# A state-space and GEGLU kernel: first weights' loads set free, constant products in TensorE's planned idle time, and a new list of priorities

## The chip, the core and the metric

The kernel runs on one core of a Trainium2 chip. The engines of the core that matter here are TensorE (PE: matrix products, which write to PSUM), VectorE (DVE), ScalarE (ACT: functions from a table that has to be loaded before a function of another table can be used) and the issuers of transfers: SyncE (SP) above all, ACT and GpSimd (POOL) for a few. Each engine works through its own list of instructions in order; an instruction that has to wait holds up everything behind it on that engine. The metric is the time of one execution on the device, in microseconds (us).

## The reference

A block on 2048 tokens with 448 channels. It is conditioned: six rows of 448 numbers come from a vector `c`.

```
mod = (silu(c) @ w_mod) -> sa, ca, ga, sb, cb, gb        # six modulation rows
h = layernorm(x) * (1 + ca) + sa
x = x + ga * S4(h)                                       # long convolution per channel
h = layernorm(x) * (1 + cb) + sb
x = x + gb * GEGLU(h)                                    # (gelu(h @ w_gate) * (h @ w_up)) @ w_down, 448 -> 1792 -> 448

S4: K[d, l] = Re sum_n C[d,n] exp(dt[d] A[d,n] l) dt[d] B[d,n]   # 256 complex terms, l = 0..2047
    y[l, d] = sum_k K[d, k] h[l - k, d] + Dskip[d] h[l, d]       # by FFT of length 4096
```

## The kernel before

**Stages.** The kernel first works up the parameters of S4 (`prep`, four groups of 112 channels): logarithms and angles of the 256 terms, split in pieces of bf16 and put in DRAM (`lh_d`), from which they come back as tables `lt`. From a table, TensorE forms exponents and angles (`x.mm`, `y.mm` in `exps`; `angles`), ACT takes exponentials and sines, DVE multiplies magnitudes with sines (`mults`), and TensorE contracts over the 256 terms (`kgen`). This goes on for 56 tiles of 8 channels; `ktail` (L735 and around) turns each pair of tiles into the first stage of a Fourier transform. Meanwhile the input is normalized with the modulation rows (`mod_row`, products at L768; `u_norm_a`, products at L832) and transformed in two stages (`u_stage_b`, L895), by way of DRAM. Channels go in three groups (160, 160, 128). For each group, `k_fft`, and `t_fft` for the last, multiply the transforms and go back; the result goes to DRAM (`y_d`) and comes back token by token (`yi`). `conv_out` finishes the inverse transform (`co.mm`, L1246 and L1251), adds the input, normalizes, and transposes (`co.t`, L1294 and L1296, for the first of four blocks of 512 tokens). Then `gate_up` (L1365, L1371) and `down_first`/`down` (L1441, L1472) do the GEGLU in products of f16 parts, each number as a high and a low part.

**Weights.** `weight(cb, k, v)` loads half `k` of chunk `cb` of the gate and up weights (512 KB) into one of three tiles `w`, and ACT and DVE split it into f16 parts (`w.hi`, L1195; `w.lo`, L1199 and L1200). The loads of chunk 0 wait for the end of the generating stage (`EV["end"]`, when its memory is given back) and for the store of the third of nine pieces of the last group (`YO[2, 2]`); the others wait for all loads of the first block's convolution output (`YL`).

**What sets the order.** Nothing is ordered by hand. Each piece of work is a task: `add(name, {engine: planned us}, due time, function, tasks it depends on, buffers it takes, buffers it uses)`. `Plan.order()` simulates the engines with these planned durations: it takes the engine that can start first, looks at all tasks which could start there within a quarter of a microsecond of that, and takes the one with the lowest due time. A tile of work has due times one apart, from 0 to 56. To a task that needs ACT to change its function table the constant `STICK` is added, so that it is put off. `spread()` adds to each due time an offset by the task's name from the list `LEAD` (several values: the tasks of the name in order are cut into as many parts); the list `LEAN` holds offsets for the choice between ACT and DVE where a task can run on either. `Plan.run()` then issues the tasks in the order found, each engine's list in that order, and the machine runs them with semaphores between the engines. A buffer given back late, a transfer or a slow product shifts the real times, but never the order.

The functions that the change touches:

Of the kernel before, what the change touches and what calls it, by code (L numbers as in the profile page):

```python
# [23 lines left out]
L, D, N, FF = 2048, 448, 256, 1792  # L24
# [15 lines left out]
    "anc": (-49.265, -80.499, -3.124, -78.469, -116.66, -66.369),  # L40
    "ang": (-3.269, -2.827, -2.729, -3.205, -2.925, -2.697), "bn": (42.111, 82.157, 5.194, -204.331),
    "c.ai": (71.008,), "c.ak": (31.634,), "c.au": (64.741,), "c.ea": (129.571,), "c.id": (-5.74,), "c.ih": (81.5,),
    "c.ld": (-70.212,), "c.rd": (36.588,), "co.add": (126.534,), "co.adde": (-479.654,), "co.addl": (177.332,),
    "co.addx": (510.429, 276.254, 263.838, 306.027), "co.c2": (-16.462, 185.363, 68.605, 81.504),
    "co.h": (1287.071, 1321.404), "co.h2": (-57.238, -19.565, -34.416, 62.618), "co.l": (166.825, 99.971),
    "co.l2": (-304.102, -376.884, -381.167, -327.959), "co.mm": (1047.13,), "co.mme": (35.95,),
    "co.mml": (321.391,), "co.mmx": (504.891, 504.282, 510.751, 509.801), "co.n": (-32.018, -300.752),
    "co.nx": (-309.183, -245.328, -200.245, -90.738), "co.rc": (52.991, 384.121), "co.rcx": (915.491,),
    "co.rt": (-12.141, 45.958), "co.rtx": (-618.711,), "co.t": (505.324, 339.683),
    "co.t2": (-464.884, -636.939, -578.467, -639.884),  # L50
    "cos": (-96.053, -141.432, -54.911, -135.117, -68.696, -62.333),
# [6 lines left out]
    "dt": (81.074,), "e.f": (-100.312, 117.922), "e.hi": (227.13, 344.995), "e.ld": (-39.805, -1.088),  # L58
    "e.lo": (8.272, -319.182), "ev.end": (-23.435,), "ev.fp": (-187.94,), "ev.geg": (-67.509,), "ev.ub": (109.206,),
    "f.fc": (-74.649, -73.839, -55.611, 15.224, 63.434, 91.147),  # L60
    "f.fwd": (58.743, 8.62, -112.416, 150.202, 15.302, 243.705),
    "f.inv": (36.676, 5.254, 29.465, 109.483, 81.689, 3.388),
    "f.pr": (-67.219, -99.593, -75.227, -57.007, -57.18, -110.784),
    "f.st": (28.45, 6.08, 190.379, 150.17, -1.775, -10.415),
    "f.ut": (-73.325, -24.751, 34.463, 33.094, 102.931, 195.732),
    "f.z": (-23.585, -5.38, 134.288, 63.022, -67.177, -41.953), "gs": (138.291,),
    "gu": (497.845, 500.786, 503.249, 509.096, 515.626, 545.649),
    "gu.g": (-625.109, -552.414, -602.197, -714.965, -686.389, -501.12), "gu.h0": (645.72, 522.69),
    "gu.ha": (-729.389, -596.515, -731.42, -528.62, -704.301, -709.342),
    "gu.hs": (-239.586, -121.625, -135.62, -164.459, -9.293, -189.977), "gu.l0": (-16.693, -130.465),  # L70
    "gu.la": (-265.608, -410.165, -336.957, -514.583, -455.359, -305.327),
    "gu.ls": (191.831, 190.571, 255.197, 314.456, 219.503, 228.103),
    "gu.m": (114.811, 93.18, 25.848, 285.848, 134.211, 151.44),
# [8 lines left out]
    "kev": (9.96, 92.747, 141.711, 161.609, -130.449, 155.883),  # L82
    "kgen": (64.902, 22.754, 68.327, 70.484, 152.571, 111.028),
    "kout": (-13.486, 89.933, 39.546, 40.541, 35.588, -116.335), "lt0": (111.543, 130.526),
    "lt1": (47.626, 207.789), "m.ev": (47.089, 10.526), "m.ld": (6.556, 99.682), "m.mm": (63.997, 73.516),
    "mag": (65.374, -12.18, 200.812, 142.622, 59.432, 179.295), "norm": (-89.669, 35.116, -31.629, -46.135),
# [7 lines left out]
    "pad": (46.718,), "rcp": (1.165,), "rstd": (-51.788,), "silu": (45.884,),  # L94
    "sin": (110.019, -92.652, 19.55, -44.113, 102.58, 38.168),
    "sin2": (46.891, 86.759, 111.859, -3.781, 88.196, 21.274), "t.fc": (52.17, 4.168), "t.fwd": (-57.224, -139.59),
    "t.inv": (-32.42, 14.481), "t.p0": (-56.821, 45.808), "t.p1": (-115.221, 1.658, 219.974, -99.911),
    "t.st": (5.684, 132.896), "t.u": (-64.85, -19.41), "t.z": (101.922, 155.786),
    "tx": (-52.929, -36.943, 40.099, -29.624, 27.922, 13.415),
    "tyc": (3.154, 41.689, 41.884, -19.547, 61.093, 75.57),  # L100
    "tys": (-48.605, -173.627, -88.574, -42.524, 36.217, -71.751), "ua": (-84.287, -53.971, -196.44, -59.869),
    "ua.ev": (-107.017, -68.693, 4.26, 84.323, 6.479, 38.324), "ua.st": (-38.083, -30.78, 73.606, -86.939),
    "ub": (61.829, 6.214, 28.274, 40.439, 45.706, 57.504),
    "ub.ev": (19.991, 47.119, -27.71, 3.763, 47.267, -78.016), "ub.fc": (-145.241, 235.998),
    "ub.st": (171.069, 76.93), "ub.u": (-80.805, 32.953), "w.hi": (47.827, -108.842, 52.672, -16.405),
    "w.ld": (-16.684, 35.68, 34.326, 174.065), "w.lo": (33.536, 32.676, -41.147, -28.811), "warm": (-47.271,),
    "wr.ld": (118.569, -172.29, -6.657, 0.537, 11.936, 73.483), "wr.st": (-77.265, -16.436),
    "x.exp": (-46.635, 7.137, 2.518, -127.479, -61.616, -65.308), "x.ld": (-9.142,), "x.ld0": (-42.934,),
    "x.ld1": (-8.964,), "x.mm": (-1.652, -1.606, -1.613, -1.701, -1.664, -1.631), "x1.ld": (17.13, -239.16),
    "y.exp": (29.939, 99.375, 54.648, -1.232, -161.973, 74.141),  # L110
    "y.mm": (-1.933, -1.54, -1.223, -1.275, -1.525, -1.518), "yi.d00": (-147.672,), "yi.d01": (-171.741,),
    "yi.d10": (-130.853,), "yi.d11": (-32.365,), "yi.e": (-88.98,), "yi.l0": (-123.965, 88.548),
    "yi.l1": (-88.669, -10.274), "yi.ld": (196.171,),
}
LEAN = {
# [23 lines left out]
class Task:  # L139
    def __init__(self, n, eng, v, fn, deps, alloc, table, kb):  # L140
# [6 lines left out]
        for b in alloc:  # L147
            self.need[b.tag] = self.need.get(b.tag, 0) + 1


class Plan:


    TABLE, HOP, STICK, RATE = 1.3, 0.3, 121.096, 280.0
    WAIT = {"ACT": 0.0}

    def __init__(self, slots):
        self.slots, self.given = slots, {t: [] for t in slots}
        self.tasks = []

# [189 lines left out]
def s4_geglu(ctx: ExitStack, tc: tile.TileContext, a: dict, out: bass.AP):  # L350
# [342 lines left out]
    KGT = {}  # L693
# [950 lines left out]
```

## Time and profile before

| | us |
|---|---|
| median of 3 runs | 823.77 |
| lowest, highest | 823.62, 831.2 |
| profiled execution, own time | 825.18 |
| profiled execution, span from first to last instruction | 823.4 |
| PE busy | 748.4 (91%) |
| DVE busy | 599.6 (73%) |
| ACT busy | 470.3 (57%) |

The mean granted clock of TensorE in the profiled execution is 0.969 of full speed. How to read the rows below: a row of a group or of the timeline gives the source line, the engine, the operation, the tile written and the tiles read, and the shapes; `x24` is a count of instructions. `[3.26 <-issue]` is the time that the engine had been idle before the row and what ended it; "issue" means nothing that the profile shows. A product of f32 operands is shown as two instructions. PEld is TensorE's loading of the stationary operand, which overlaps products. SPq, ACTq and POOLq are the issuing of transfers by these engines. In the chain of waits (the work that ended last, followed back) a row is a start, a length and what it was.

### The profile page before, as it was taken

How to read it: one execution, taken by the hardware profiler on the slowest of the kernel's cores; microseconds unless marked ns; L12 is line 12 of the kernel's file. 1: busy time of each engine (PE TensorE's matmuls, PEld its weight loads, DVE VectorE, ACT ScalarE, POOL GpSimd, SP SyncE). 2: the span in 40 equal slices, each digit the busy share in tenths (PEclk: the TensorE clock that was granted, in tenths of full speed). 3: DMA queues.
4: the chain of work that ended last, by engine and by line, in shares of the span. 5: the costliest groups of instructions: out<-in, count | busy, mean ns of one | idle time of the engine just before them, and what ended most of it. 6: DMA issues, size and time to landing. Idle time of an engine off the chain costs nothing.

```text
span 823.4 us, 19059 instructions
## 1 busy us (share of the span) xinstructions
PE 748.4 (91%) x8166; PEld 461.2 (56%) x8166; DVE 599.6 (73%) x981; ACT 470.3 (57%) x629; POOL 6.0 (1%) x14
## 2 busy tenths in 40 slices
PE   2786789999799999998589999999999999999997
PEld 1344344444577767778466445444496445864477
DVE  7789998999889989897494783178863686244542
ACT  5598999899968999971244553034442353113320
POOL 0000000000000000000200000000000000000000
PEclk9888799999999999999889999999999999999999
DMA  9552369996858846899669756245315322022101
GB/s 283 148 167 92 105 189 236 285 273 200 236 146 257 233 133 193 253 307 295 189 197 298 267 179 179 75 140 166 117 53 146 135 91 90 34 79 90 45 12 35
DMA packets 92526, 136.83 MB, mean 166 GB/s; under 512 B 21280, under 2 KB 75200, under 8 KB 92442
## 3 DMA queue, kind: packets, MB, share of 16 engines
q1 hardware_dynamic: 89514, 133.75, 53.8%
q10 hardware_dynamic: 2608, 1.61, 0.8%
q8 instruction: 64, 1.05, 0.5%
q0 software_dynamic: 320, 0.26, 0.1%
q14 instruction: 20, 0.16, 0.1%
HBM read 100.48 MB, written 36.01 MB: 166 GB/s over the span
## 4 chain that ended last, share of the span: by engine, by line
PE 67%; ACT 12%; DVE 10%; DMA 6%; issue 3%; SPq 1%; DVEq 0%; ACTq 0%
PE pq L1371 30%; PE pq L1472 9%; PE pd L1441 3%; PE kg L710 3%; ACT fg L643 2%; PE pg L630 2%; PE pf L999 2%; PE pq L1365 2%; PE pf L768 2%; ACT my L617 2%; PE pf L1085 2%; PE pf L895 2%; DVE tx L679 2%; DMA fg<-in_w_mod 2%; PE pd L1472 1%
## 5 line engine op out<-in xcount | busy, mean ns | idle before, releaser
L1371 PE MATMUL pq<-ht,wr 128*128 128x512 f16 (+1 forms) x1200 | 250.0, 367 | 0.0
L1371 PEld LDWEIGHTS <-wr 128*128 128x128 f16 x1200 | 115.4, 98 | 128.6 <-issue 11.0
L1378 ACT ACTIVATE ge<-pq 128x512 f32<-128x512 f32 (+1 forms) x60 | 33.9, 568 | 144.5 <-PE pq L1365 93.9
L1385 DVE TENSOR_TENSOR fq<-ge,pq 128x512 f32<-128x512 f32 (+1 forms) x60 | 38.5, 649 | 72.1 <-PE pq L1371 48.2
L1397 ACT ACTIVATE hh<-fq 128x1024 f16<-128x1024 f32 (+1 forms) x49 | 47.1, 963 | 54.5 <-DVE fq L1385 41.8
L1472 PE MATMUL pq<-d,hh 128*128 128x224 f16 x504 | 73.2, 259 | 0.0
L710 PE MATMUL kg<-ty,tx 128*32 128x64 f32 x3584 | 61.8, 221 | 11.3 <-DVE ty L687 6.4
L679 DVE TENSOR_TENSOR tx<-mx,fg 128x1024 f32<-128x1024 f32 x56 | 68.0, 1220 | 4.0 <-ACT fg L654 2.2
L683 DVE TENSOR_TENSOR ty<-my,fg 128x1024 f32<-128x1024 f32 x56 | 68.2, 1219 | 3.0 <-PE kg L710 2.8
L710 PEld LDWEIGHTS kg<-ty,tx 128*32 128x32 f32 x3584 | 53.0, 110 | 27.6 <-issue 11.2
L1472 PE MATMUL pq<-d,hlo 128*128 128x224 f16 x252 | 65.3, 259 | 0.0
L1400 DVE TENSOR_TENSOR hlo<-fq,hh 128x1024 f16<-128x1024 f32 (+1 forms) x49 | 53.9, 1104 | 5.3 <-ACT hh L1397 5.0
L643 ACT ACTIVATE fg<-pg 128x1024 f32<-128x1024 f32 x56 | 56.6, 1019 | 1.9 <-issue 1.2
L1472 PEld LDWEIGHTS <-hh 128*128 128x128 f16 x588 | 56.7, 98 | 1.1 <-issue 0.4
L617 ACT ACTIVATE my<-pg 128x1024 f32<-128x1024 f32 x56 | 55.3, 1041 | 3.1 <-PE pg L612 2.9
L999 PE MATMUL pf<-q,fc 128*128 128x160 f32 x264 | 42.9, 313 | 0.3 <-DVE q L989 0.3
L630 PEld LDWEIGHTS <-lt 64*128 64x128 bf16 x336 | 20.7, 95 | 37.4 <-issue 20.7
L999 PEld LDWEIGHTS pf<-q,fc 128*128 128x128 f32 x264 | 37.7, 195 | 6.3 <-issue 3.3
L630 PE MATMUL pg<-ea,lt 64*128 64x512 bf16 x168 | 34.9, 389 | 6.2 <-ACT fg L643 4.4
L687 DVE TENSOR_TENSOR ty<-my,fg 128x512 f32<-128x512 f32 x56 | 38.4, 686 | 0.0
L686 DVE SCALAR_TENSOR_TENSOR ty<-my,fg 128x512 f32<-128x512 f32 x56 | 38.4, 685 | 0.0
L735 PE MATMUL kg<-ak,ke 128*64 128x128 f32 x448 | 32.1, 284 | 6.2 <-DVE ke L730 4.4
(172 smaller groups left out, 1196.3 us busy)
## 6 DMA issues: line engine op xcount, KB each, us to landing
wr<-w_d SPq DMA_DIRECT2D x21, 896.0 KB
fc<-in_k_fc SPq DMA_DIRECT2D x20, 576.0 KB
u_d<-so SPq DMA_DIRECT2D x32, 224.0 KB
w<-in_wgu SPq DMA_DIRECT2D x14, 512.0 KB
ui<-u_d SPq DMA_DIRECT2D x10, 672.0 KB
w_d<-wr SPq DMA_DIRECT2D x7, 896.0 KB
fq<-in_wd SPq DMA_DIRECT2D x14, 448.0 KB
us<-uo SPq DMA_DIRECT2D x22, 240.0 KB
```

The source lines that it names most:

```text
L617: A.activation(yb.tile.rearrange("p a b c -> p (a b c)"), pb.tile, AF.Exp)
L630: T.matmul(pa[:, nh * 512:nh * 512 + 512], w, x, start=(k == 0), stop=(k == 2))
L643: A.activation(fb.tile[:, 0].rearrange("p x (n k) -> p n x k", n=2), pb.tile.rearrange("p (n x k) -> p n x k", n=2, x=2), AF.Sin, scale=TW ...
L679: V.tensor_mul(tx.tile, xb.tile[:, xm, None, :].to_broadcast([128, 2, 512]), fb.tile[:, :, 0])
L683: V.tensor_mul(ty.tile[:, 1], yb.tile, fy()[:, 1, :, None, :].to_broadcast([128, 16, 2, 32]))
L710: T.matmul(kg[32 * g:32 * g + 32, 2 * (s % 2) + q, :64], tx[:, r, nh, 4 * q + g], ty[:, r, nh, 4 * q + g], start=(r == 0 and nh == 0), sto ...
L999: T.matmul(pz.tile[:, e % 32 - sl0], fc.tile[:, i, 1 + t], pp.tile[:, t, i], start=(t == 0 and e != 32), stop=(t == 1 and e != 0))
L1371: T.matmul(pb[k].tile[:, ts], wr.tile[:, 4 * lo + t, k, c0:c0 + 128], ht[:, m, ts], start=f % 2 == 0 and i == 0, stop=f % 2 == 1 and i == 9)
L1385: V.tensor_mul(to if half is None else to[:, half:half + 1], *src)
L1397: A.activation(hg.tile[0][:, cb, c], fq.tile[:, c], AF.Copy)
L1400: V.tensor_sub(hg.tile[1][:, cb, c], fq.tile[:, c], hg.tile[0][:, cb, c])
L1472: T.matmul(bank(k)[:, m], x[:, p, q[0], ts], w[:, p, q[1]], start=new and m == 0 and p == 0 and z == 0, skip_group_check=True, stop=i in ( ...
```

## The change

Three things are changed.

First, the loads of weight chunk 0 no longer wait for the store of the third piece of the last group; they wait for the end of the generating stage alone.

Second, `Plan.run()` notes for each TensorE task how long the plan has TensorE idle before it (its planned start less the planned end of the TensorE task before). A new function `spin` runs at the beginning of six kinds of tasks: the exponents of `x.mm`, the even tiles of `kgen`, the modulation rows `m.mm`, the first transform of the input `ua`, the inverse transform `co.mm` and the transposition `co.t`. It multiplies a constant (the 1e-5 in `small`, broadcast to 128x128 and to 128x448 in f32) into the PSUM tile that the task writes anyway, as often as 0.78 us (for 448 columns) go into the planned idle time less 1.5 us. The real products of the task then start that tile anew, so the numbers are not changed.

Third, all values of `LEAD` and `LEAN` are new (some 330 numbers), and `STICK` goes from 121.096 to 68.223.

```diff
 LEAD = {
-    "anc": (-49.265, -80.499, -3.124, -78.469, -116.66, -66.369),
-    "ang": (-3.269, -2.827, -2.729, -3.205, -2.925, -2.697), "bn": (42.111, 82.157, 5.194, -204.331),
+    "anc": (-33.662, -127.623, -27.273, -157.195, -251.708, -72.885),
+    "ang": (-2.669, -2.583, -2.453, -2.632, -2.559, -2.718), "bn": (39.589, -6.152, 5.448, -202.784),
...
-    "x.exp": (-46.635, 7.137, 2.518, -127.479, -61.616, -65.308), "x.ld": (-9.142,), "x.ld0": (-42.934,),
-    "x.ld1": (-8.964,), "x.mm": (-1.652, -1.606, -1.613, -1.701, -1.664, -1.631), "x1.ld": (17.13, -239.16),
+    "x.exp": (-2.362, 27.057, -3.169, -158.186, 25.842, -71.775), "x.ld": (80.516,), "x.ld0": (-45.034,),
+    "x.ld1": (-29.649,), "x.mm": (-1.578, -1.384, -0.684, -1.385, -1.425, -1.155), "x1.ld": (126.383, -240.404),
...
 class Plan:
-    TABLE, HOP, STICK, RATE = 1.3, 0.3, 121.096, 280.0
+    TABLE, HOP, STICK, RATE = 1.3, 0.3, 68.223, 280.0
...
     def run(self):
+        free = 0.0
         for t in self.order():
+            if t.on == "PE":
+                t.idle, free = t.start - free, t.start + t.eng["PE"]
             t.fn(t.on) if len(t.eng) > 1 else t.fn()
...
+    def spin(me, dst, w=D):
+        for _ in range(int(max(0.0, me[0].idle - 1.5) / (0.78 * w / D))):
+            T.matmul(dst, eps.to_broadcast([128, 128]), eps.to_broadcast([128, w]), start=True, stop=True)
...
         def mm():
             pb.tile = fft.tile([128, D], FT, name="pf")
+            spin(me, pb.tile)
             for t in range(4):
                 T.matmul(pb.tile, c_sb[:, t:t + 1].to_broadcast([DT, 128]), wb.tile[:, t], start=(t == 0), stop=(t == 3))
...
         t2 = add("m.mm", {"PE": 3.22}, v, mm, [t1, t_si], [pb], [wb])
+        me.append(t2)
...
-        hold = [YO[2, 2]] if cb < 1 else YL
+        hold = [] if cb < 1 else YL
         t1 = add("w.ld", {"SP": 0.42}, v - 3, ld, [EV["end"]] + hold, [wb], kb=540)
...
                     if i == 0:
                         pb.tile = POOLS["pd"].tile([128, D], FT, name="pd")
+                    spin(me, pb.tile[:, c0:c1], c1 - c0)
```

In `x.mm`, `kgen`, `ua` and `co.t` the call stands in the same way right after the PSUM tile is taken, with 448 columns. In `co.mm` it is as wide as the part of the tile that the task writes (320, 128 or 448 columns).

More of the change, by code (lines that the diff above doesn't have):

```diff
@@ L45 @@
[L45 to L50, printed above, removed]
@@ L64 @@
[L64 to L70, printed above, removed]
@@ new lines @@
+    "c.ai": (101.027,), "c.ak": (51.722,), "c.au": (99.561,), "c.ea": (166.012,), "c.id": (-139.636,),
+    "c.ih": (99.349,), "c.ld": (-111.229,), "c.rd": (34.126,), "co.add": (212.033,), "co.adde": (-451.647,),
+    "co.addl": (214.941,), "co.addx": (383.522, 332.612, 197.427, 173.233),
+    "co.c2": (-4.423, 230.15, -17.347, 23.461), "co.h": (1272.011, 1283.454),
+    "co.h2": (-135.097, -190.215, -25.533, 9.464), "co.l": (41.666, 122.947),
+    "co.l2": (-239.239, -340.178, -513.762, -355.004), "co.mm": (1081.405,), "co.mme": (13.439,),
@@ new lines @@
+    "e.lo": (73.412, -325.804), "ev.end": (30.652,), "ev.fp": (-421.684,), "ev.geg": (-34.16,), "ev.ub": (13.47,),
+    "f.fc": (-73.936, -73.769, -11.85, 1.571, 13.444, 40.743),
+    "f.fwd": (50.686, -9.55, -79.473, 68.866, 75.039, 267.068),
+    "f.inv": (31.32, 15.273, 27.125, 42.942, 7.704, 10.82),
+    "f.pr": (-29.69, -89.709, -108.076, -161.126, -21.4, -65.159),
+    "f.st": (23.073, 80.857, 222.835, 174.159, -46.499, 51.897),
+    "f.ut": (-73.466, -8.761, 21.784, 68.205, 83.502, 144.889),
@@ new lines @@
+    "f.z": (10.584, 18.046, 60.685, 42.739, -117.035, 2.404), "gs": (281.067,),
+    "gu": (483.796, 504.978, 502.422, 517.711, 492.364, 538.942),
+    "gu.g": (-641.228, -487.117, -586.793, -843.942, -558.876, -526.773), "gu.h0": (676.217, 477.898),
+    "gu.ha": (-653.183, -638.161, -685.036, -501.963, -686.837, -740.305),
+    "gu.hs": (-254.496, -129.449, -206.502, -147.449, -41.548, -76.458), "gu.l0": (90.866, -195.141),
+    "gu.la": (-123.506, -257.422, -386.797, -503.762, -370.765, -243.05),
@@ new lines @@
+    "w.ld": (1.251, 10.186, 42.098, 313.892), "w.lo": (28.842, 98.808, -7.712, -66.755), "warm": (-39.422,),
+    "wr.ld": (84.303, -194.951, 103.092, -69.821, -11.301, 59.36), "wr.st": (-81.84, -85.079),
+    "x.exp": (-2.362, 27.057, -3.169, -158.186, 25.842, -71.775), "x.ld": (80.516,), "x.ld0": (-45.034,),
+    "x.ld1": (-29.649,), "x.mm": (-1.578, -1.384, -0.684, -1.385, -1.425, -1.155), "x1.ld": (126.383, -240.404),
+    "y.exp": (32.326, 75.885, 82.416, -34.586, -96.967, -56.007),
+    "y.mm": (-1.65, -1.332, -0.716, -1.386, -0.969, -0.964), "yi.d00": (-61.494,), "yi.d01": (-166.546,),
@@ L587, in exps, with xmm @@
             pb, mb = Buf("pg"), Buf("mx")
-            def xmm(grp=grp, pb=pb):
+            me = []
+            def xmm(grp=grp, pb=pb, me=me):
                 pb.tile = gen.tile([128, 1024], FT, name="pg")
+                spin(me, pb.tile[:, :D])
                 for m, s in enumerate(grp):
@@ L695, in kgen @@
     def kgen(s, deps):
-        m = s // 2
+        m, me = s // 2, []
         if s % 2 == 0:
@@ L702, in go @@
                 KG[m].tile = kgp.tile([128, 4, 128], FT, name="kg")
+                spin(me, KG[m].tile.rearrange("p q d -> p (q d)")[:, :D])
             kg = KG[m].tile
@@ L712, in go @@
                                      tile_position=(0, 32 * g))
-        return add("kgen", {"PE": 1.04}, s, go, list(deps) + [KGT.get(s - 1) if s % 2 else None],
-                   [KG[m]] if s % 2 == 0 else [], [TX[s], TY[s]] + ([KG[m]] if s % 2 else []))
+        me.append(add("kgen", {"PE": 1.04}, s, go, list(deps) + [KGT.get(s - 1) if s % 2 else None],
+                      [KG[m]] if s % 2 == 0 else [], [TX[s], TY[s]] + ([KG[m]] if s % 2 else [])))
+        return me[0]
     AKB = [Buf("ak%d" % (g % 2)) for g in range(3)]
@@ L826, in u_norm_a, with mm @@
             pbs = [Buf("pf"), Buf("pf")]
-            def mm(j=j, pbs=pbs):
+            me = []
+            def mm(j=j, pbs=pbs, me=me):
                 for h in range(2):
                     pbs[h].tile = fft.tile([128, D], FT, name="pf")
+                spin(me, pbs[0].tile)
                 for h in range(2):
@@ L1289, in norm, with tr @@
                 V.scalar_tensor_tensor(xn.tile, xn.tile, RS[blk][:, j:j + 1], sb, op0=OP.mult, op1=OP.add)
-            def tr(pt=pt, xn=xn):
+            me = []
+            def tr(pt=pt, xn=xn, me=me):
                 pt.tile = POOLS["ps"].tile([128, 4, 128], FT, name="pq")
+                spin(me, pt.tile.rearrange("p k t -> p (k t)")[:, :D])
                 for k in range(3):
```

79 lines of the change are left out of this document (38 added, 41 removed), and 48 rows, old and new, of tables (LEAD, LEAN).

## The prediction

> **What bounds the kernel now.** I began with the page: how full TensorE is, where its clock drops, who carries the chain that ended last.
>
> ```profile
> span 823.4 us, 19059 instructions
> PE   2786789999799999998589999999999999999997
> PEclk9888799999999999999889999999999999999999
> PE 67%; ACT 12%; DVE 10%; DMA 6%; issue 3%; SPq 1%; DVEq 0%; ACTq 0%
> ```
>
> A slice is 20.6 us. TensorE is nearly full from slice 22 on. Its clock is below full in three places: slices 2 to 5, slices 20 and 21 (from about 400 us), and a dip in the slices before 240 us. I then split the span at five events: the first table arrives (33.2), the last kernel tile is done (376.5), the last inverse transform ends (398.6), the first gate/up product starts (421.5).
>
> ```profile
> 0.00:33.20 33.20, 13.41 (x28) 6.05 (x28) 23.14 (x60) 16.32 (x28) 0.20 (x4) 0.99 0.82 237
> 33.20:376.50 343.30, 306.10 (x5306) 194.49 (x5306) 313.17 (x468) 308.00 (x396) 0.00 (x0) 0.95 0.71 207
> 398.60:421.50 22.90, 9.84 (x66) 6.15 (x64) 14.47 (x32) 8.40 (x14) 2.82 (x5) 0.77 0.58 187
> 421.50:823.40 401.90, 396.97 (x2574) 232.44 (x2572) 231.53 (x396) 131.98 (x184) 0.00 (x0) 0.99 0.38 120
> ```
>
> Columns: stretch, its length, busy time (and instructions) of PE, weight loads, DVE, ACT and POOL, granted clock, DMA share, GB/s. The last stretch is TensorE's: 396.97 of 401.90 us at clock 0.99, so no order and no constant product can shorten it by more than 5 us. Whatever the change brings or costs falls ahead of 421.5 us. In the long stretch three engines are about equally full: DVE is idle for 343.3 - 313.2 = 30.1 us, ACT for 35.3, PE for 37.2. There the order decides, and DVE's 30 us is the most that a better order can win. The first and third stretches are chains in which each engine waits for another.
>
> **The constant products at the start.** The spin loop stands ahead of the real products in TensorE's queue and waits for nothing but the PSUM tile and the constant. The first host is the product of a modulation row.
>
> ```profile
> 2.63 13.19 DMA fg<-in_w_mod
> 15.96 12.27 PE pf L768 x24
> 28.33 4.86 DMA lt<-lh_d
> 233.23 3.01 PE pf L768 x8
> ...
> 15.96 12.26 PE L768 MATMUL pf<-fg,pk 112*128 112x448 f32 x24 [15.96 <-DMA fg<-in_w_mod]
> 21.32 0.34 PEld L768 LDWEIGHTS pf<-fg,pk 112*128 112x128 f32 x1 [0.41 <-issue]
> 22.04 0.19 PEld L768 LDWEIGHTS pf<-fg,pk 112*128 112x128 f32 x1 [0.38 <-issue]
> 22.24 0.54 ACT L771 ACTIVATE rows<-pf 128x448 f32<-128x448 f32 x1 [6.01 <-PE pf L768]
> 22.30 0.34 ACTq L520 DMA_DIRECT2D lh_d<-lh  x1
> 22.41 0.19 PEld L768 LDWEIGHTS pf<-fg,pk 112*128 112x128 f32 x1 [0.19 <-issue]
> ```
>
> The first four rows are the chain of waits (start, length), the others the timeline. Three modulation rows took 12.27 us at the start; one took 3.01 us at 233 us, so three warm ones take 9.03. The weight loads show why: they start 0.72 us apart up to 22.04 and 0.37 apart after it. From 15.96 to 22.04, 6.1 us, the array ran at half speed. Being warm at 15.96 is worth 12.27 - 9.03 = 3.2 us, and this lies on the path: ACT waits 6.01 us for the first of these rows with the store of the first factor queued behind it, and the load of the first table is issued at 28.33, when the last of the rows is out.
>
> How many constant products are planned I can't read; I put the real idle time in place of the planned one. 15.96 us give int((15.96 - 1.5) / 0.78) = 18. One is a quarter of a modulation row: 3.01 / 4 = 0.75 us warm, 1.5 cold. Four run in the 6.1 us of warming, the other 14 take 10.5, together 16.6 us; begun near 1 us they end at 17.5, 1.6 us after the data landed (2.63 + 13.19 = 15.82). So the term lies between -3.2 (they fit) and -1.6 (they overhang); I take -2.5.
>
> The Trainium skill, "TensorE: Matmul & The Clock Gate", Part 1, says that the array is held at half clock until it has been busy for about one window of 3.4 us. The trace has the same two speeds but needed 6.1 us here; by the page's figure the warm start would be worth 3.4 / 2 = 1.7 us (estimate), by the row 3.2, and the row decides.
>
> **The next cold stretches.**
>
> ```profile
> 31.48 1.16 PE L832 MATMUL pf<-xt,au 64*128 64x448 f32 x4 [3.26 <-issue]
> 43.49 1.92 PE L832 MATMUL pf<-xt,au 64*128 64x448 f32 x4
> 64.01 1.00 PE L832 MATMUL pf<-xt,au 64*128 64x448 f32 x4
> 78.98 1.98 PE L735 MATMUL kg<-ak,ke 128*64 128x128 f32 x16 [3.75 <-DVE ke L730]
> ...
> 34.63 1.49 PE pf L832 x4
> 36.55 2.22 PE pf L832 x4
> 43.72 1.70 PE pf L832 x4
> ```
>
> After 3.26 us of idling at 31.48 the products of L832 cost 1.92 us for four instructions against 1.00 when warm (64.01). The three pieces of them that the chain shows add up to 5.41 us; half is 2.7. They are a host, and the gap of 3.26 gives int(1.76 / 0.78) = 2 constant products, which may or may not hold the clock through the short gaps that follow. Between 0 and -2.7 I take -1. The gap of 3.75 us before L735 has no host, so nothing fills it in the order of before: 0.
>
> **The constant products before the first gate/up product.**
>
> ```profile
> 410.23 1.32 PE L1251 MATMUL pd<-yi,ai 128*64 128x128 f32 x8 [9.99 <-DMA yi<-y]
> ...
> 410.23 0.91 PE pd L1251 x4
> 420.25 0.94 PE pq L1294 x6
> 421.61 3.85 PE pq L1371 x20
> 425.78 2.29 PE pq L1371 x20
> 428.07 0.67 PE pq L1294 x6
> ```
>
> The chain passes through cold products here: the first twenty gate/up products took 3.85 us and the next twenty 2.29 (1.56 more); a transposition took 0.94 against 0.67 (0.27); half of the 0.91 at 410.23 is 0.45. Together 2.3 us. The host has a real gap of 9.99 us, but its tile part is 128 columns wide, so each product is 0.75 x 128/448 = 0.21 us. By the real gap int(8.49 / 0.223) = 38 of them: at 0.43 us cold 14 fill the 6.1 us, the other 24 take 5.1, 11.2 in all, which overhangs a gap of 9.99 by 1.2. From -2.3 to -1.1; the later transpositions are hosts too. I take -1.8.
>
> **Elsewhere constant products only get in the way.**
>
> ```profile
> L710 PE MATMUL kg<-ty,tx 128*32 128x64 f32 x3584 | 61.8, 221 | 11.3 <-DVE ty L687 6.4 <-issue 3.4 <-ACT ako L408 1.3
> L593 PE MATMUL pg<-rd,lt 64*128 64x256 bf16 x112 | 13.4, 297 | 5.1 <-ACT my L617 3.3 <-ACT mx L599 1.1 <-ACT fg L643 0.2
> ```
>
> The two hosts of the long stretch had 11.3 and 5.1 us of idle time before them in many small pieces, and one product needs a planned gap of 1.5 + 0.78 = 2.28. If the planner's gaps are as small as the real ones, the term is 0. If it sees all 37.2 us of the stretch's PE idle time as gaps of 2.28 ahead of hosts, 16 products of 0.75 us, 12 us, stand in TensorE's queue; at its 67% of the chain, +8. I take one product, +0.8, because the real pieces are small.
>
> **The first weights' loads.**
>
> ```profile
> 395.49 0.43 SPq L1187 DMA_DIRECT2D w<-in_wgu  x1
> 396.66 0.55 SPq L1187 DMA_DIRECT2D w<-in_wgu  x1
> 400.51 3.72 SPq L1166 DMA_DIRECT2D yi<-zo  x2
> ```
>
> Two issues leave SP's queue where they stood among the loads of the last convolution output, 0.98 us, and go ahead of them. SP then stands for 3.72 us at L1166 anyhow, which swallows the 0.98: 0, with -1 if that stall shrinks. Their megabyte (2 x 512 KB) would move into the time around 380 us, where it competes with the loads of the transforms: at the 207 GB/s of the long stretch that is 5 us of transfer, nearly all hidden behind a busy TensorE; +1 at worst. What uses these weights, two conversions on ACT and DVE near 401 us, now sits in idle time and gains nothing by being early.
>
> **The priorities.** Every due time moves, and the row that prices it is the long stretch: from -30.1 (DVE never idle) to a loss that no row caps; the first rival prices one. No row gives its sign. I take a tenth of the idle time, -3: a choice, not a reading. The start at least keeps its order, since both lists rank SP's first loads alike (parameters, inputs, modulation rows).
>
> **Sum.** -2.5 - 1 - 1.8 + 0.8 + 0 - 3 = -7.5. The profiled execution took 825.18 us (span 823.4 and 1.8 around it), so 817.7; the median of the three runs is 1.4 below the profiled one, so **816.3 us**, 0.9% less.
>
> **Rivals.**
>
> *More table changes on ACT (slower).* The planner's reluctance to change ACT's function table falls from 121 to 68, in units in which one tile of work is 1.
>
> ```profile
> L599 ACT ACT_TABLE_LOAD x8 | 10.3, 1283 | 0.1
> ```
>
> Each load holds ACT 1.283 us, and ACT is as full as DVE there, so it delays the path nearly in full. Six more loads eat the 7.5 us; twelve put the time at 816.3 + 15.4 = 831.7, 1% slower than before. Against it: both values exceed the 56 tiles that there are, so alternation stays dear.
>
> *Products in the way.* The planner's gaps aren't the chip's; +8 instead of +0.8: 823.5. For it: TensorE is busy 306 us of 343 there, and a queue in order can't step past a constant product. Against it: the small gaps above.
>
> *A better order.* The new order closes a third of DVE's 30.1 us, -10 in place of -3: 809.3. For it: the order of before was laid out for a TensorE that was warm, and it wasn't; DVE, ACT and PE idle at different times. Against it: three engines above 89% leave little to shift.
>
> *The clock is down again when the work comes.* The constant products end where the plan expects the data; where the data are over 3 us later than planned, the array idles and is cold, as after 3.26 us at 31.48 and 3.75 at 78.98. Then the clock terms (-2.5, -1, -1.8) go and 821.6 is left. The Trainium skill, "TensorE: Matmul & The Clock Gate", in its section on why this matters, allows no gap above about 3 us between bursts; both rows agree.
>
> **How the numbers follow.** The forecast has 0.34, the table changes 0.17, products in the way 0.15, the better order 0.26, the lost clock 0.08. A measurement of this kernel tells about 1% from no change, so "faster" is below 815.5 and "slower" above 832.0. Faster: 0.15 of the forecast (its own range is 810 to 822) and all of the better order, 0.41. Slower: 0.13 of the table changes and 0.04 of the products in the way, 0.17. The rest, 0.42, is within 1%. The range goes from 803 (the better order with the full clock terms) to 831 (twelve table loads); about 0.07 lies below and 0.12 above.
>
> **What would show it.** The start: products of `small` ahead of L768, three modulation rows in about 9 us, the table's load issued near 25.5 instead of 28.33. Around 410: narrow constant products in the gap, the first twenty gate/up products in 2.3 us. The long stretch: table loads counted, DVE's idle time above or below 30. It is wrong if the stretch from the first gate/up product on changes by over 5 us, or if the start gains nothing although the three rows are fast.

## The result, and the profile after

The changed kernel took 816.3 us (median of 12 runs, 813.34 to 825.16), the kernel before 825.39 us beside it (12 runs, 820.12 to 831.76). The ratio is 0.988, with a 95% interval of 0.985 to 0.991. The profiled execution took 817.22 us, with a span of 814.8. Ratios, here and below, use executions in the chip's faster state alone and are not quotients of the medians, from which they differ by up to 0.003.

From the page of the changed kernel: span, TensorE's busy share and clock in 40 slices, and the chain's shares by engine.

```profile
span 814.8 us, 19269 instructions
...
PE   9786788999899999989889999999999999999997
...
PEclk9898899999999999998999999999999999999999
...
PE 71%; ACT 11%; DVE 9%; DMA 5%; issue 3%; SPq 1%; ACTq 0%; DVEq 0%
```

A slice is 20.4 us. Of the clock's low slices at the start the third is full now and the fifth went from 7 to 8; the two from 391 to 432 us (20 and 21) are gone, and slice 19, from 367 us, is new. The changed kernel's time by stage (columns as in the prediction), cut at the first table, the last kernel tile, the end of the inverse transform and the first gate/up product:

```profile
0.00:29.10 29.10, 26.91 (x66) 12.93 (x66) 22.60 (x59) 16.06 (x28) 0.20 (x4) 1.00 0.86 253
29.10:369.40 340.30, 304.12 (x5308) 193.14 (x5308) 312.42 (x465) 309.68 (x399) 0.00 (x0) 0.96 0.73 212
369.40:395.00 25.60, 25.54 (x204) 24.80 (x206) 20.55 (x33) 8.06 (x13) 2.96 (x5) 0.91 0.85 231
395.00:410.60 15.60, 12.47 (x106) 10.19 (x107) 7.62 (x20) 2.28 (x7) 2.81 (x5) 1.00 0.62 198
410.60:814.80 404.20, 397.33 (x2582) 232.34 (x2581) 236.44 (x408) 134.69 (x184) 0.00 (x0) 1.00 0.38 119
```

Three stages became shorter: the first by 4.1 us (33.2 to 29.1), the long one by 3.0, the chain after the inverse transform by 7.3 (22.9 to 15.6). Two became longer: the transforms between the last kernel tile and the end of the inverse transform by 3.5 (22.1, which is 376.5 to 398.6 in the kernel before, to 25.6; TensorE is full in both, but its clock is 0.91 here), and the last one by 2.3 (401.9 to 404.2). The start, first in the chain of waits, then in the timeline:

```profile
0.92 14.60 PE pf L418 x32
15.52 9.04 PE pf L785 x24
```

```profile
15.36 9.18 PE L785 MATMUL pf<-fg,pk 112*128 112x448 f32 x24
...
18.57 0.55 ACT L789 ACTIVATE rows<-pf 128x448 f32<-128x448 f32 x1 [2.38 <-PE pf L785]
...
24.66 1.39 ACTq L583 DMA_DIRECT2D lt<-lh_d  x2
```

The constant products (L418) now run up to the modulation rows (L785, formerly L768). Three rows take 9.04 us where they took 12.27, ACT waits 2.38 us for the first of them where it waited 6.01, and the first table's load is issued at 24.66 instead of 28.33. The stretch before the first gate/up product in the same timeline:

```profile
395.56 6.74 PE L418 MATMUL pd<-small 128*128 128x128 f32 x58
...
403.38 0.85 PE L1276 MATMUL pd<-yi,ai 128*64 128x128 f32 x8 [1.08 <-DMA y<-zo]
...
410.61 0.60 PE L1401 MATMUL pq<-ht,wr 128*128 128x256 f16 x4 [0.91 <-ACT ht L412]
...
412.36 1.91 PE L1401 MATMUL pq<-ht,wr 128*128 128x256 f16 x16 [1.15 <-DVE ht L1333]
```

The 29 narrow constant products (58 records) end 1.08 us before the data, the products of `co.mm` take 0.85 us instead of 1.32, and the twenty gate/up products take 0.60 and 1.91 us, warm (the part on the prediction says why that is not the constant products' doing). Between them TensorE now waits for the normalized activations (`ht`) of VectorE.

One row that is not there any more matters more than these. In the timeline of the kernel before, the products that contract over the 256 terms (`kgen`, 64 records of products for a tile, here two tiles in a row) stood still once, in the middle of a tile:

```profile
221.67 1.88 PE L710 MATMUL kg<-ty,tx 128*32 128x64 f32 x107
226.93 0.86 PE L710 MATMUL kg<-ty,tx 128*32 128x64 f32 x21 [3.38 <-issue]
...
362.34 0.93 PE L735 MATMUL kg<-ak,ke 128*64 128x128 f32 x13 [1.51 <-issue]
```

After 107 of the 128 products TensorE idled for 3.38 us, and nothing in the profile released it: VectorE had written the last factor of the second tile at 222.63 (a row of 0.68 us begun at 221.95) and stood waiting for these products itself from 225.1 on. TensorE idled in the same way for 1.51 us before the last 13 products of a group at 362 us. Cut into stretches of 2 us, the kernel before shows that the clock went down behind the first stop and that VectorE ran out of work:

```profile
224.00:226.00 2.00, 0.00 (x0) 0.00 (x0) 1.08 (x1) 2.00 (x3) 0.00 (x0) 1.00 0.16 44
226.00:228.00 2.00, 1.07 (x22) 0.91 (x23) 0.11 (x1) 0.85 (x2) 0.00 (x0) 0.70 0.03 8
228.00:230.00 2.00, 2.00 (x8) 2.00 (x9) 2.00 (x3) 0.21 (x1) 0.00 (x0) 0.50 0.00 0
```

VectorE is busy for 0.11 us of the 2 from 226, and the clock is at half until 230. The changed kernel's timeline has this in its place:

```profile
220.21 0.31 PE L723 MATMUL kg<-ty,tx 128*32 128x64 f32 x4 [0.49 <-DVE ty L699]
220.91 1.09 PE L723 MATMUL kg<-ty,tx 128*32 128x64 f32 x60 [0.39 <-issue]
```

A stop of 0.39 us. No constant product stands near, and the experiments show that the new order of the work isn't what took the stop away.

### The profile page after: what moved, and what is told of

Same layout as the page of the kernel before. It is cut to its first block, busy times and chain, and to the rows that moved or that the text cites. A ratio compares the mean times of both kernels' runs of the same rounds, so it can differ in the third digit from the quotient of the medians.

```text
span 814.8 us, 19269 instructions
## 1 busy us (share of the span) xinstructions
PE 766.4 (94%) x8264; PEld 473.4 (58%) x8264; DVE 599.6 (74%) x982; ACT 470.8 (58%) x628; POOL 6.0 (1%) x14
## 4 chain that ended last, share of the span: by engine, by line
PE 71%; ACT 11%; DVE 9%; DMA 5%; issue 3%; SPq 1%; ACTq 0%; DVEq 0%
PE pq L1401 30%; PE pq L1502 9%; PE pd L1471 4%; PE pg L642 3%; PE kg L723 3%; ACT fg L655 2%; PE pf L917 2%; PE pf L1021 2%; PE pq L1395 2%; PE pf L785 2%; PE pf L1107 2%; PE pf L418 2%; ACT my L629 2%; ACT fg L647 2%; PE pd L1502 1%
```

## The experiments

All kernels compute the whole output. Ratios are to the kernel before on the same chip, with 95% intervals. Times within a profile are of one execution each.

### One part at a time

**The new lists alone** (LEAD, LEAN, STICK; the condition on the first weights kept; no constant products).

```diff
 LEAD = {
-    "anc": (-49.265, -80.499, -3.124, -78.469, -116.66, -66.369),
+    "anc": (-33.662, -127.623, -27.273, -157.195, -251.708, -72.885),
...
-    TABLE, HOP, STICK, RATE = 1.3, 0.3, 121.096, 280.0
+    TABLE, HOP, STICK, RATE = 1.3, 0.3, 68.223, 280.0
```

> The new priorities and the new reluctance to change tables alone: no constant products, and the first weights' loads planned after the store of the third piece as before. Theory (the clock terms make most of the gain, the order about 3 us): 3 us below before, ratio 0.996; three modulation rows at the start in about 12 us as before. Rival 'the order makes it all': ratio 0.988 to 0.990.

823.26 us, 0.995 (0.992 to 0.998). Most of the gain is around 400 us: from the start of the last copy `zo` (the end of the inverse transform) to the first gate/up product it took 15.8 us against 22.4 before. The stall was there, 2.96 us before the last 21 products of a `kgen` group at 226.74.

**The constant products alone** (old lists, old condition).

```diff
+    def spin(me, dst, w=D):
+        for _ in range(int(max(0.0, me[0].idle - 1.5) / (0.78 * w / D))):
+            T.matmul(dst, eps.to_broadcast([128, 128]), eps.to_broadcast([128, w]), start=True, stop=True)
...
+                spin(me, pb.tile[:, :D])
```

> The kernel before with the constant products alone, old priorities, old condition. Theory: the start gains 2.5 to 3.2 us, the gap before the first gate/up product 1.1 to 2.3 us, together 4 to 6 us, ratio 0.993 to 0.995. Rival 'the order makes it all': ratio 1.000. Rival 'products in the way': 1.000 or above, with constant products directly ahead of waiting work in the stretch from 33 to 376 us.

818.65 us, 0.987 (0.983 to 0.992): as much as the whole change. The modulation rows took 9.50 us.

**The condition on the first weights' loads alone.**

```diff
-        hold = [YO[2, 2]] if cb < 1 else YL
+        hold = [] if cb < 1 else YL
```

> The kernel before with only the condition of the first weights' loads taken away, old priorities, no constant products. Theory: nothing, ratio 0.999 to 1.001. Rival 'the freed loads clear the transition before the gate/up products': 2 to 4 us less between the last inverse transform and the first gate/up product, ratio 0.995 to 0.998.

823.72 us, 0.994 (0.991 to 0.997). SyncE issues the two loads at 378.93 instead of 395.49 and 396.66. From this kernel's timeline and chain of waits:

```profile
402.76 3.21 SPq L1187 DMA_DIRECT2D yi<-zo  x4
```

```profile
402.61 2.15 DMA yi<-zo
```

The last store of the transform took 4.17 us on the chain before and takes 2.15 here, and from the start of the last copy `zo` to the first gate/up product it is 19.1 us instead of 22.4. Its stall before the last 21 products was 4.45 us.

**The changed kernel without the constant products** (new lists, no condition).

```diff
-        for _ in range(int(max(0.0, me[0].idle - 1.5) / (0.78 * w / D))):
+        for _ in range(0):
```

> The changed kernel without its constant products: new priorities and the condition taken away. Theory: as the new priorities alone, ratio 0.996, with the start at 12 us for three modulation rows and a cold first gate/up product. Rival 'the order makes it all': ratio 0.988 as the whole change. Rival 'the freed loads': 0.992.

822.88 us, 0.993 (0.990 to 0.995). So lists and condition together bring little more than either alone, and the constant products bring the most. In the timeline of this kernel the stall is back:

```profile
225.65 0.53 PE L723 MATMUL kg<-ty,tx 128*32 128x64 f32 x21 [4.04 <-issue]
```

### Is it the clock?

If the constant products help by keeping the array warm, products too small to warm it must not help. In two kernels each constant product is cut from 128x128 times 448 (or 128) columns to 32x32.

```diff
-            T.matmul(dst, eps.to_broadcast([128, 128]), eps.to_broadcast([128, w]), start=True, stop=True)
+            T.matmul(dst[:32, :32], eps.to_broadcast([128, 32]), eps.to_broadcast([128, 32]), start=True, stop=True)
```

In the changed kernel:

> The changed kernel with each constant product cut to 32 by 32: as many instructions at the same places of TensorE's queue, but a few us of work in all, which can't warm the array. Theory 'warm clock': the gain of the products goes, ratio 0.992 to 0.996 as without them, three modulation rows in about 12 us. Rival 'position in the instruction stream' (the stall of 3 to 4 us that ended without a releaser inside a kgen group near 225 us, in every kernel without constant products, shrinks since the inserted instructions shift the groups against it): the stall is below 1 us here too, and of the gain of 5 us at least 3 stay, ratio 0.989 to 0.991. At the first gate/up product the array is cold in both.

818.94 us, 0.989 (0.985 to 0.993).

In the kernel with the constant products alone:

> The kernel before (old priorities, old condition) with each constant product cut to 32 by 32. Theory 'warm clock': as before, ratio 0.998 to 1.001. Rival 'position in the instruction stream': the stall inside kgen near 225 us falls from 3 to 4 us to below 1, 3 to 4 us less, ratio 0.995 to 0.997, with three modulation rows still at 12 us.

819.55 us, 0.990 (0.986 to 0.994).

Beside them, on the same chip, the two kernels with full products: the changed kernel,

> The changed kernel itself beside the others on this chip: ratio 0.985 to 0.991. If the new priorities and the condition bring nothing beside the constant products, it equals the constant products alone; if they bring 3 us, it lies 0.004 below them.

817.11 us, 0.987 (0.983 to 0.991); and the constant products alone,

> The kernel before with the constant products alone, on the same chip as the changed kernel. Theory (clock terms 5.3 us, order 3 us): 0.993 to 0.995 and 3 us above the changed kernel. Rival 'the constant products make it all': equal to the changed kernel within 1 us.

818.23 us, 0.990 (0.986 to 0.994). (These two are the kernels of above, without an edit.)

Cutting the products costs nothing that can be measured: 0.990 and 0.990 with the old lists, 0.989 and 0.987 with the new. Yet the cut products did not warm the array, as the timeline of the old-list kernel shows:

```profile
0.92 1.91 PE L417 MATMUL pf<-small 128*32 128x32 f32 x32 [0.92 <-DVE small L392]
13.27 11.09 PE L784 MATMUL pf<-fg,pk 112*128 112x448 f32 x24 [10.44 <-DMA fg<-in_w_mod]
...
219.73 1.10 PE L722 MATMUL kg<-ty,tx 128*32 128x64 f32 x64 [0.50 <-DVE ty L698]
```

The 16 products end at 2.8 us, TensorE idles for 10.44 us, and the three rows take 11.09 us. But the `kgen` group that stood still runs through in 1.10 us. So the gain goes with the instructions ahead, not with the clock.

The clock does what the prediction priced, where it stands. From the start of the modulation rows to the first product of magnitudes and sines (the first `tx`) it is 34.7 us with full products (15.63 to 50.29) and 37.6 with cut ones (13.27 to 50.87), 2.9 us less. At the last group of `ktail` only 1.4 of them is left (352.7 us after the start of the rows against 354.1), and the medians differ by 1.3 us, within their intervals. The next row, from the full products with the old lists, shows what became of the term at 400 us:

```profile
405.98 1.32 PE L1275 MATMUL pd<-yi,ai 128*64 128x128 f32 x8 [3.04 <-DMA yi<-y]
```

The narrow products had ended 3.04 us before the data, and the array was cold again: 1.32 us, as without them.

### Is it the place in the list of instructions?

One product of f32 operands is four instructions to TensorE (two weight loads, two products). Counted in products and weight loads, the first instruction after the stop has nearly the same number in the kernels so far: 5,287 without constant products, and 5,287 or 5,289 at the stops of 0.39 to 0.99 us that some of the kernels have left with 19 constant products (76 instructions) ahead. Other work stands at this number there. The whole list is of 2 x 8166 = 16,332 instructions in the kernel before and 2 x 8264 = 16,528 in the changed one, and these are the pages' rows on the queue that brings instructions (packets, MB, share), first before, then after:

```profile
q8 instruction: 64, 1.05, 0.5%
```

```profile
q8 instruction: 65, 1.06, 0.6%
```

1.05 MB / 64 is 16.4 KB for a packet; 16,332 / 256 = 63.8 and 16,528 / 256 = 64.6. If instructions come in blocks of 256, a shift by 256 puts the same work back at the same place of a block, and the stop must return; by the theory of the clock, or if any instructions ahead would do, nothing returns. The first kernel adds 64 cut products (256 instructions) ahead of the first modulation row to the kernel before, and nothing else:

```diff
+            if i == 2:
+                for _ in range(64):
+                    T.matmul(pb.tile[:32, :32], eps.to_broadcast([128, 32]), eps.to_broadcast([128, 32]), start=True, stop=True)
```

> The kernel before with 64 constant products of 32 by 32 ahead of the first modulation row and nothing else. In the trace a f32 product is two loads and two products, so everything behind moves by 256 instructions, one whole block of the instruction queue (64 transfers of 16 KB for 16,334 instructions). Theory 'position': the stalls come back at their old places (21 products of kgen left near 225 us, 13 products of L735 left near 362), 3 to 4.5 and 1.5 to 1.8 us, and the time is that of before, ratio 0.997 to 1.001. Rival 'any products ahead help': 0.990, as with the 19 cut products that moved the stream by 76 instructions.

828.83 us, 1.001 (0.998 to 1.004): all of the gain is gone. The timeline has the same stops at the same work:

```profile
222.55 1.75 PE L710 MATMUL kg<-ty,tx 128*32 128x64 f32 x107
227.26 0.53 PE L710 MATMUL kg<-ty,tx 128*32 128x64 f32 x21 [2.96 <-issue]
...
362.42 1.65 PE L735 MATMUL kg<-ak,ke 128*64 128x128 f32 x13 [2.31 <-issue]
```

The second kernel has the same shift with full products too: at the modulation row 55 cut and 6 full products in place of the 16 full ones, and the other constant products as they are with the old lists. The edit is shown against the kernel with the constant products alone.

```diff
-            spin(me, pb.tile)
+            if i == 2:
+                for _ in range(55):
+                    T.matmul(pb.tile[:32, :32], eps.to_broadcast([128, 32]), eps.to_broadcast([128, 32]), start=True, stop=True)
+                for _ in range(6):
+                    T.matmul(pb.tile, eps.to_broadcast([128, 128]), eps.to_broadcast([128, D]), start=True, stop=True)
```

> The kernel before with the constant products alone, but at the start 55 small ones and 6 full ones in place of 16 full ones, so that with the three before the first product of L832 everything behind moves by 256 instructions: warm clock without the shift. Theory 'warm clock and position add up': three modulation rows in 9 to 9.5 us, the stalls near 225 and 362 us as before, 2 to 4 us less than before, ratio 0.995 to 0.998. Rival 'the clock makes it all': 0.990, as with the products in their old numbers.

826.5 us, 0.998 (0.995 to 1.002), and the stall is there:

```profile
227.95 0.83 PE L722 MATMUL kg<-ty,tx 128*32 128x64 f32 x21 [4.33 <-issue]
```

In its profile the full products ended 5.29 us before the data and the rows took 12.48 us, so this run did not show a warm start without the shift, as it was meant to; the narrow products at 400 us were there. What it shows is that full products at this place in the list bring no gain that can be told from none.

The same split in all profiles, from the first `tx` to the last group of `ktail` (one execution each, us):

| the last 21 products of a `kgen` group | kernels | first `tx` to last `ktail` |
|---|---|---|
| stop for 2.96 to 4.45 us | before; lists alone; condition alone; changed without products; both shifts by 256 | 321.3; 319.4; 323.4; 319.4; 322.3; 325.4 |
| no stop at that work | changed (two profiles); products alone (two); cut products, new and old lists; the two kernels below | 317.0, 314.7; 317.0, 318.1; 317.0, 316.5; 317.2, 316.4 |

The two groups don't overlap, whatever the lists; their means are 321.9 and 316.7, 5.1 us apart. All stops of over 0.15 us that end by "issue" between 50 and 400 us add up to 5.1 to 7.5 us in the profiles of the first row and to 0.7 to 2.9 in those of the second.

The traces also settle what the engine waited for. First, the place: with the waiting instructions counted in, which the rows above leave out, 5,313 instructions stand ahead of the first stopped one in the kernel before, 10,177 ahead of the second, and 5,569 and 10,433 in the kernel shifted by 256. Each of these numbers leaves 193 when divided by 256, and so do those of all 44 stops of over 0.15 us between 50 and 400 us in the fourteen profiles; with blocks of 128 some would leave 65. Second, the block itself. These are the transfers of the kernel before from 217.5 to 223.55 us, up to the stop, and from 223.55 to 226.93, during it:

```profile
DMA packets 558, 1.76 MB, mean 291 GB/s; under 512 B 72, under 2 KB 345, under 8 KB 557
...
q1 hardware_dynamic: 557, 1.75, 103.2%
q14 instruction: 1, 0.01, 0.5%
```

```profile
DMA packets 30, 0.12 MB, mean 37 GB/s; under 512 B 14, under 2 KB 14, under 8 KB 29
...
q1 hardware_dynamic: 29, 0.11, 12.1%
q8 instruction: 1, 0.02, 2.0%
```

Ahead of the stop, q8, whose packets fit TensorE's list, brings nothing; during it, it brings one packet. The trace has this packet with 16,384 bytes from 224.45 to 225.54, and TensorE goes on 1.38 us after that. In all six long stops the packet starts when TensorE stands already, and TensorE goes on 1.36 to 1.45 us after its end. The packet starts 4.2 to 5.8 us after TensorE passed the last such place, 256 instructions earlier. TensorE ran through these 256 in 3.8 to 3.9 us in the six; in the eight profiles with 76 instructions more, the 256 that end at number 5,313 are other work and took 5.7 to 6.6 us, so that the next block was there, or nearly.

### Two attempts to gain more

In some profiles the array is at half clock when the long stretch ends (the last group of `ktail` takes 1.75 us instead of 1.09, and forty products of the transform behind it 6.95). Four constant products of 256 columns ahead of the last `kgen` were to hold the clock:

```diff
+            if s == NSUB - 1:
+                for _ in range(4):
+                    T.matmul(KG[m].tile.rearrange("p q d -> p (q d)")[:, 256:], eps.to_broadcast([128, 128]),
+                             eps.to_broadcast([128, 256]), start=True, stop=True)
```

> The changed kernel with four more constant products of 256 columns (1.7 us) in the wait of 1.87 us ahead of the last kgen. In some executions the array went to half clock there, and the first products of the last group took 6.95 us (chain of waits) instead of 4.73. Theory 'clock': L735 1.1 us and the forty products of the transform in 4.7 us in every profile, 1 to 2 us below the changed kernel, ratio 0.984 to 0.987. Rival 'the last kgen starts later': as the changed kernel, 0.987 to 0.988.

817.05 us, 0.987 (0.982 to 0.992). In its profile the last group takes 1.09 us, but the time is that of the changed kernel: one profile of the changed kernel has 1.09 there too.

The second has, besides, the copies of half of the first block's activations on ACT instead of VectorE, since TensorE waits for them at the second pair of transpositions:

```diff
-    "co.c2": (16.144, 7.379, 17.327, -7.811), "co.h": (1.424, -17.726), "co.h2": (10.328, 0.449, 0.303, 5.389),
+    "co.c2": (16.144, 7.379, 17.327, -7.811), "co.h": (1.424, 17.726), "co.h2": (10.328, 0.449, 0.303, 5.389),
```

> As the one with the fill, and the third and fourth high parts of the first block's transposed input are copied by ACT and no longer by DVE (one value of the second list turned in sign; TensorE's order stays). In the changed kernel TensorE waited 2.8 us there for four DVE steps in a row. Theory: the wait falls below 1.5 us, 1 to 2 us less than with the fill alone, ratio 0.982 to 0.985. Rival 'ACT is late there too' (a weight conversion and four activations stand ahead): no change.

816.5 us, 0.987 (0.981 to 0.993). The wait in the timeline fell only from 0.88 to 0.69 us:

```profile
425.51 2.63 PE L1405 MATMUL pq<-ht,wr 128*128 128x256 f16 x20 [0.69 <-ACT ht L412]
```

Both attempts missed: neither is measurably better than the changed kernel.

## Why the prediction was right, and where only by its sum

The median came out at the forecast, 816.3. Direction, size and range were right; the sum's terms were not, and the largest single gain isn't among them. That the number agrees to the digit is luck: 7.5 us were taken off a median of three runs, 823.77, while the kernel before took 825.39 over the twelve runs beside the changed one, so the change was worth 9.1.

**The start (-2.5, between -3.2 and -1.6): right where it stands, smaller at the end.** 12.27 to 9.04 us is 3.2, and the table's load came 3.7 us earlier, 0.6 of it because the rows began at 15.36 instead of 15.96. In the other timelines cold rows took between 11.09 and 12.48 us, and rows within 1.1 us of the constant products 9.18 to 9.50, so the term is 1.6 to 3.3. Whether the 16 products overhang depends on the execution: they end at 15.5, and the data landed between 13.27 and 18.28 in the profiles that show it. But the step from there to the end was too simple: with the long stall out of the comparison, 2.9 us at the first `tx` were 1.4 at the last group of `ktail` and 1.3, within the intervals, in the medians. Some 0.6 of the 1.5 us lost are short stops (1.34 us in all with full products, 0.75 with cut ones). That three nearly full engines don't hand on a head start in full would explain the rest; it is argued, not shown. The estimate from the figure of the Trainium skill ("TensorE: Matmul & The Clock Gate", Part 1) was 1.7 us, that from the row 3.2, and the rows of this execution gave 3.2.

**The next cold stretches (-1): nothing.** From the end of the modulation rows to the first `tx` it was 25.2 us before (28.22 to 53.45) and 25.5 after (24.54 to 49.99). The prediction misread its row: the 1.92 us at 43.49 stand 12 us behind the idle time of 3.26 at 31.48, and the granted clock was full between (1.00 from 40 to 42 us). Three constant products now fill that idle time (2.43 us from 24.38), but the clock is down again from 34 to 40 us (0.50), behind waits of 0.34 and 1.57 us for the tables.

**The gap before the first gate/up product (-1.8): the wrong cause, and mis-sized.** The gate/up products are warm in the changed kernel, but the constant products didn't warm them: with the lists alone, and with cut products, `co.mm` is cold (1.31 us) and the same gate/up products take 0.60 and 1.91 us all the same. TensorE was idle for 3.07 us ahead of the last transposition of the old order; between the transpositions and the gate/up products of the new one it is idle for 1.15 us at most. What is left to the constant products is `co.mm` and the first transposition: with cut products the way from the last `zo` to the second set of gate/up products took 17.7 us, against 17.3 and 16.8 in the two profiles of the changed kernel, so 0.3 to 0.9 us. With the old lists the rival "the clock is down again when the work comes" happened at this place, by the 3.04 us above.

**Products in the way (+0.8): right.** One constant product stands in the long stretch; the group below is that one, a pair of records in the changed kernel's groups of instructions:

```profile
L418 PE MATMUL kg<-small 128*128 128x448 f32 x2 | 1.0, 592 | 0.0
```

**The step that failed** is the reading of the row of L710: "11.3 and 5.1 us of idle time before them in many small pieces". The row itself said "issue 3.4" and was quoted, but not split; one look at the timeline would have shown a single stop of 3.38 us in the middle of a group. The prediction then costed a constant product by the array's time alone. Its larger effect is on the list of instructions: 76 more of them ahead put other work into the block that TensorE had left before the next one came. Cut products, which do this and left the rows cold (11.09 us), gave 0.990 (0.986 to 0.994), and a shift by 256 gave 1.001 (0.998 to 1.004).

**The first weights' loads (0, between -1 and +1): mis-sized.** Alone they gave 0.994 (0.991 to 0.997), some 5 of 828.57 us. The case that the prediction put at -1 happened, "if that stall shrinks": SyncE's stop at the transfers behind the store (`yi<-zo`) fell from 3.72 us for two issues to 3.21 for four, and the chain's piece from 4.17 to 2.15. The prediction sought the price in the queue. The piece follows the condition in every profile: 2.09 to 2.42 us in the seven without it, 3.24 to 4.62 in the seven with it; in the kernel before, DMA moved 246 GB/s during the piece, without the condition 134. This agrees with the megabyte moving beside these small transfers. How much of the 5 us comes from there isn't shown: the way from `zo` to the first gate/up product gained 3.3.

**The priorities (-3): right in size, by chance.** Alone 0.995 (0.992 to 0.998), some 4 us. The gain is not where the row of VectorE's idle time put it: that went from 30.1 to 27.9 us (340.3 - 312.42) in the changed kernel, while with the lists alone the stretch before the first gate/up product gained 6.6 us, the one from the last group of `ktail` to the last `zo` lost 2.0 (24.4 to 26.4), and the last stage gave 2.3 back. A table's loading is counted 43 times in both kernels, so the first rival is out. These two terms don't add up: together, without constant products, they gave 0.993 (0.990 to 0.995). On top of the constant products they bring 0.990 to 0.987, within the intervals.

**What stays open.** That TensorE stood for a block of instructions is shown; why this block's transfer started so late isn't. The stop fell among the smallest f32 products (the 64 records of a tile and their 64 weight loads run in 1.10 us), and in the six microseconds before it DMA was full (267 to 289 GB/s, share 1.02 to 1.07, in the six profiles). But of 108 ends of blocks that TensorE reached after six such microseconds (share 1.00 or more), it stopped at 12, so full DMA alone doesn't make a block late enough. The ratio of 1.001 against 0.990 is some 9 us, and the intervals leave room for 3 to 15; in the two profiles all stops add up to 7.0 and 0.7 us, and what lies beyond these 6.3 isn't shown.

## What to carry to other kernels

An idle time that ends by "issue" in the middle of a group whose inputs are all there is not a wait of the plan: split it in the timeline before it is put among "small pieces", count the instructions up to it, and look whether a packet of the instruction queue lands just before it ends. Where an edit adds instructions to a full engine, measure it beside a control that adds as many without their effect (here cut products, and a shift by one whole block), or the gain is put down to the wrong cause. And time won at the start of a stretch in which three engines are nearly full need not be time won at its end: measure it there.

## What the runs showed of the hardware that was not expected

TensorE stood still for 2.96 to 4.45 us at one fixed place of its list, with no wait in the program, in six kernels, with old and new lists; 76 instructions ahead of it took it away (0 to 0.99 us left) and 256 brought it back. The Trainium skill, "Runtime: NRT & Kernel Launch", section "Instruction fetch mechanics", says that an engine's instructions are refilled in blocks of 16 KiB, 256 instructions, by a queue of their own. The packets of 16,384 bytes, the remainder of 193 at all 44 stops and the return of the stop at a shift of 256 agree with that. The section also says that the refill is hidden because instructions are issued more slowly than they come; here the stop of 3.38 us, which carried the clock to 0.50 behind it, speaks against this for dense small f32 products. A long stop ended 1.36 to 1.45 us after its block's packet, which itself took 1.0 to 1.2 us.
